# Routing and plan in measured parts beside the first expert units, all splits on VectorE in another order, and a drain of GpSimd

## The chip, the cores and the metric

The kernel runs on one core of a Trainium2 chip. The metric is the device time of one execution in microseconds (us), as the median of several runs. It takes 1409.32 us before the change (three runs, 1408.02 to 1411.92).

## What is computed

Three layers stand behind each other, all float32, for 4608 tokens of width 512:

```python
# attention with softmax over features (q) and over the sequence (k); x is [4608, 512]
kv = einsum('bhsd,bhse->bhde', k_s, v);  x = einsum('bhsd,bhde->bhse', q_s, kv)
# dense layer, 512 -> 2048 -> 512
r = maximum(x @ w_in, 0);  x = (s * (r * r) + b) @ w_out
# experts: 8, each 512 -> 1024 -> 512; a token goes to one of them
logits = xn @ en.T / tau;  expert_idx = argmax(logits);  gate = max of softmax(logits)
for e in range(8):
    h = maximum(x[mask] @ w1[e], 0);  out[mask] = gate[mask, None] * (h @ w2[e])
```

## The kernel before, in words

Precision: a float32 product is made of three matmuls in the fast type `float32r`: every operand is split into a high part (ScalarE copies and rounds it) and a low part (a subtraction, mostly on VectorE), and high x high, low x high and high x low are summed in PSUM. An expert's weights are split anew for each unit.

Stages: up to about 940 us the attention and the dense layer run in 12 blocks of 384 tokens. When a block of the dense layer is done, `route` (line 534) finds the expert of each of its tokens: 24 dot products on VectorE (3 groups of 128 tokens x 8 experts, lines 541 to 543), norms (with a power on GpSimd, line 504), the softmax, two small matmuls that count places (lines 579, 580), and three indirect DMAs from GpSimd that scatter (token, gate) into a table `tab` sorted by expert (line 597). `plan` (line 728) then works out which rows of the table and which expert each unit takes. `plan(True)` serves units 0 to 7 from the first 10 blocks and runs before the experts begin. `plan(False)` serves the later units and needs the routing of the last block (`NB - 1` = 11).

From 940 us on the expert stage runs 20 units, counted from 0 here and in the code: 18 units of 256 tokens (`FULL` = 18) and two of 128 tokens (units 18 and 19, `STAT` = 20), and more behind a condition that these inputs don't meet. A unit (`unit`, line 693) is two halves on TensorE. The first (L1, lines 688 to 690) has four quarters of 24 matmuls; each quarter's result goes through ScalarE (`hh`, line 704) and VectorE (`hl`, line 705) and then frees its PSUM buffer, of which there are two. The second half (L2, lines 715 to 717) has 48 matmuls. Between them `hook1(0..3)`, one behind each quarter of L1, and `hook2(0..3)`, at four places of L2, put the work for this unit's second weights and for the next unit into the engines' queues:

- `split(2, c)` (line 651): the four pieces of the second weights of this unit, 128 x 1024 each, a ScalarE copy (line 653) and a subtraction (line 654);
- `split(1, c)`: the four pieces of the first weights of the next unit;
- `emit_tr` (line 656): the 32 x 32 transposes of the next unit's tokens on VectorE (line 661), the ScalarE copy `xh` (line 664) and the VectorE subtraction `xl` (line 665);
- `gather` (line 622): two indirect DMAs from GpSimd that fetch the tokens of the unit after the next into `xr`;
- `deal` (line 630): 16 DMAs from SyncE that move `xr` into the layout `x` that the transposes read;
- `fetch_w1`, `fetch_w2`, `fetch_ids`: DMAs from SyncE; the weights' ones move nothing where the expert stays the same.

Each engine takes its queue in order. In the kernel before, `last_step` (line 1056) runs one step of the routing of block 11, and then of `plan(False)`, behind every hook, eight a unit: first one dot product a step, later the steps that the `yield`s in `route` and `plan` cut, with every third hook left out. While the routing runs, `split(2, 3)` has its subtraction on GpSimd, and until the plan is done `split(1, 0)` too. Unit 6 asserts that both are done, since `fetch_ids(8)` there reads the plan. `hook2` makes `split(1, i)` first and the transposes behind it, in `hook2(0)`, in unit 0 in `hook2(1)`. The first unit is begun early: `last_block` (line 964) loads, gathers, deals and splits for unit 0 beside the last dense block, and behind its last L1 (`m == NM`) does the first quarter of unit 0.

Of the kernel before, what the change touches and what calls it, by code (L numbers as in the profile page):

```python
# [8 lines left out]
F32 = mybir.dt.float32  # L9
# [4 lines left out]
ALU = mybir.AluOpType  # L14
# [7 lines left out]
E, F = 8, 1024  # L22
BT = 384
NB = NT // BT
# [8 lines left out]
FULL = 18  # L33
# [9 lines left out]
def attn_ffn_moe(ctx: ExitStack, tc: tile.TileContext, q, k, v, w_in, w_out, s_in, b_in,  # L43
# [490 lines left out]
    def route(t, nd=(3, 2)):  # L534
# [3 lines left out]
        for c in range(NC):  # L538
            yt = ysb.pop((t, c))
            for e in range(E):  # L540
                nc.vector.tensor_tensor_reduce(  # L541
                    out=junk_box[-1], in0=yt, in1=eb[:, e, :], scale=1.0, scalar=0.0,
                    op0=ALU.mult, op1=ALU.add, accum_out=dt[:, c, e:e + 1])
                n += 1
                if n == nd[k % len(nd)]:
                    n = 0
                    k += 1
                    yield
        nr = yield from norm_of(lp, sq, NC, "nr")
        nc.vector.reciprocal(out=nr, in_=nr)  # L550
        nc.vector.tensor_scalar(out=nr, in0=nr, scalar1=itau, scalar2=None, op0=ALU.mult)
        yield
        bc = lambda a: a.unsqueeze(2).to_broadcast([128, NC, E])
# [6 lines left out]
        ex = lp.tile([128, NC, E], F32, tag="ex", name="ex", bufs=1)  # L560
        nc.scalar.activation(out=ex, in_=dt, func=AF.Exp)

        pos = lp.tile([128, NC, E], F32, tag="pos", name="pos", bufs=1)
# [21 lines left out]
        ix = lp.tile([128, NC], I32, tag="ix", name="ix", bufs=2)  # L585
        nc.vector.tensor_copy(out=ix, in_=mx)
        nc.vector.tensor_tensor(out=cnt, in0=cnt, in1=pp[:, n3:n3 + E], op=ALU.add)
        py = lp.tile([128, NC, 2], I32, tag="py", name="py", bufs=2)
# [3 lines left out]
        nc.vector.tensor_copy(out=py[:, :, 0], in_=tok[:, NC * t:NC * t + NC])  # L592
        yield

# [7 lines left out]
        if t == NB - 1:  # L602
            list(scatter())
            yield
        else:
            prep.append(scatter())
# [5 lines left out]
    def parts_of(u):  # L612
        return 1 if FULL <= u < STAT else 2
# [36 lines left out]

    def split(n, c, eng=None):
        raw, hi, lo = moe[f"r{n}"][c], moe[f"h{n}"][c], moe[f"l{n}"][c]
        nc.scalar.activation(out=hi, in_=raw, func=AF.Copy)  # L653
        (eng or nc.vector).tensor_tensor(out=lo, in0=raw, in1=hi.bitcast(F32), op=ALU.subtract)  # L654

    def emit_tr(u):
        x, xf = moe["x"], moe["xf"]
        xh, xl = moe["xh"][u % 2], moe["xl"][u % 2]
        n = 128 * parts_of(u)
        xv = xf[:, :, 0:n]  # L660
        nc.vector.transpose(out=xv.rearrange("p c (g j) -> p g c j", j=32),
                            in_=x[:, 0:n // 32, :].rearrange("p g (c i) -> p g c i", c=KC))
        if n == UT:
            nc.scalar.activation(out=xh, in_=xv, func=AF.Copy)  # L664
            nc.vector.tensor_tensor(out=xl, in0=xv, in1=xh.bitcast(F32), op=ALU.subtract)  # L665
# [62 lines left out]
    def plan(first):  # L728
# [21 lines left out]
        for i in range(nb // E):  # L750
            nc.gpsimd.tensor_copy(out=eb[:, E * i:E * i + E], in_=eidx[0:1])
            nc.gpsimd.tensor_copy(out=rb[:, E * i:E * i + E], in_=segb[0:1])
        yield
        tt(out=c0, in0=cnt[0:1], in1=segb[0:1], op=ALU.subtract)
# [5 lines left out]
        cp(out=nu[:, 0:E], in_=ci)  # L760
        if not first:
            nc.vector.scalar_tensor_tensor(out=c0, in0=nu[:, 0:E], scalar=-float(UT), in1=c0,
                                           op0=ALU.mult, op1=ALU.add)
            ts(out=nu[:, E:], in0=c0, scalar1=0.0, scalar2=None, op0=ALU.is_gt)
            tt(out=rb[:, 0:E], in0=rb[:, 0:E], in1=eoff, op=ALU.add)
            nc.vector.scalar_tensor_tensor(out=rb[:, E:], in0=nu[:, 0:E], scalar=float(UT), in1=rb[:, 0:E],
                                           op0=ALU.mult, op1=ALU.add)
        yield

        for i in range(nb // E):  # L770
            src, dst = nu[:, E * i:E * i + E], c0
            for d in (1, 2, 4):
                a, z = slice(0, E - d), slice(d, E)
                o = hi[:, E * i:E * i + E] if d == 4 else dst
                if i == 0:
                    cp(out=o[:, E - d:E], in_=src[:, E - d:E])
                    tt(out=o[:, a], in0=src[:, a], in1=src[:, z], op=ALU.add)
                else:
                    cp(out=o[:, 0:d], in_=src[:, 0:d])
                    tt(out=o[:, z], in0=src[:, z], in1=src[:, a], op=ALU.add)  # L780
                src, dst = dst, c1
            if i:
                ts(out=hi[:, E:], in0=hi[:, E:], scalar1=hi[:, 0:1], scalar2=None, op0=ALU.add)
# [7 lines left out]
        nc.vector.scalar_tensor_tensor(out=rb, in0=lo, scalar=-float(UT), in1=rb, op0=ALU.mult, op1=ALU.add)  # L791
        yield
        tt(out=g3, in0=bu(uf), in1=be(lo), op=ALU.is_ge)
        tt(out=t3, in0=bu(uf), in1=be(hi), op=ALU.is_ge)
        tt(out=g3, in0=g3, in1=t3, op=ALU.subtract)
        nc.vector.tensor_reduce(out=va, in_=g3, axis=AX.X, op=ALU.add)
        tt(out=t3, in0=g3, in1=be(rb), op=ALU.mult)
        nc.vector.tensor_reduce(out=st, in_=t3, axis=AX.X, op=ALU.add)
        yield
        tt(out=t3, in0=g3, in1=be(eb), op=ALU.mult)  # L800
        nc.vector.tensor_reduce(out=ex[:, 1:], in_=t3, axis=AX.X, op=ALU.add)
        nc.vector.scalar_tensor_tensor(out=st, in0=uf, scalar=float(UT), in1=st, op0=ALU.mult, op1=ALU.add)

        ts(out=va, in0=va, scalar1=-2.0 * E * SEG, scalar2=2.0 * E * SEG, op0=ALU.mult, op1=ALU.add)
        tt(out=st, in0=st, in1=va, op=ALU.add)
        ts(out=st, in0=st, scalar1=float(E * SEG), scalar2=None, op0=ALU.min)
        yield
        ut = tp.tile([1, 3 * n + 3], I32, tag="ut" + tg, name="ut", bufs=1)
        u3 = ut[:, 0:3 * n].rearrange("p (n u) -> p n u", n=3)
        if first:  # L810
            nc.vector.memset(ex[:, 0:1], -1.0)
        else:
            cp(out=ex[:, 0:1], in_=ut_box[0][0:1, 2 * NA - 1:2 * NA])

            h0, h1 = FULL - NA, STAT - NA
            ts(out=c0[:, 0:2], in0=uf[:, h0:h1], scalar1=hi[:, 0:1], scalar2=None, op0=ALU.is_ge)
            ts(out=c1[:, 0:2], in0=c0[:, 0:2], scalar1=-float(E * SEG), scalar2=float(E * SEG),
               op0=ALU.mult, op1=ALU.add)
            tt(out=c1[:, 0:2], in0=c1[:, 0:2], in1=st[:, h0:h1], op=ALU.max)
            cp(out=ut[:, 3 * n:3 * n + 2], in_=c1[:, 0:2])  # L820
            ts(out=c0[:, 0:2], in0=c0[:, 0:2], scalar1=float(E * SEG), scalar2=None, op0=ALU.mult)
            tt(out=st[:, h0:h1], in0=c0[:, 0:2], in1=st[:, h0:h1], op=ALU.max)
            ts(out=c0[:, 0:1], in0=hi[:, 2 * E - 1:], scalar1=-2.0, scalar2=hi[:, 0:1], op0=ALU.add, op1=ALU.max)
            cp(out=ut[:, 3 * n + 2:], in_=c0[:, 0:1])
# [16 lines left out]
    with tc.manual_schedule():  # L841
# [97 lines left out]

        state = {}  # L940

# [22 lines left out]
        def last_block(m):  # L964
# [24 lines left out]
            if m == NM:  # L989
                early.append(unit_l1(0, 0))  # L990
            if m == NM + 1:
                xh, xl = rooms(2, F32R, "xh1", [128, KC, UT])
                moe["xh"].append(xh)
                moe["xl"].append(xl)
# [58 lines left out]

        steps = [0]

        def last_step():
            steps[0] += 1
            if steps[0] > NC * E and steps[0] % 3 == 0:
                return
            while last:  # L1060
                try:
                    next(last[0])
                    return
                except StopIteration:
                    last.pop(0)

        def run_unit(u, end):
# [4 lines left out]
            if more:  # L1072
                eg = fetch_w1(u + 1) if u + 1 != STAT - 1 else None
                if u + 2 < end:
                    fetch_ids(u + 2)

            def hook1(i):
                split(2, i, nc.gpsimd if len(last) > 1 and i == 3 else None)
                if i == 1 and more:
                    deal(u + 1)  # L1080
                if i == 3 and more:
                    if eg is not None:
# [3 lines left out]
                    if u + 2 == STAT - 1:  # L1086
# [4 lines left out]
                        load_w1(moe["e"], to="e1")  # L1091
                last_step()

            def trans():
                if more:
                    emit_tr(u + 1)
                    if u + 2 < end:
                        gather(u + 2)

            def hook2(i):  # L1100
                if more and parts_of(u + 1) == 2:
                    split(1, i, nc.gpsimd if last and i == 0 else None)
                if i == (1 if u == 0 else 0):
                    trans()
                last_step()

# [75 lines left out]
```

## Time and profile before

| | |
|---|---|
| median of 3 runs | 1409.32 us (1408.02 to 1411.92) |
| the profiled execution, time | 1407.17 us |
| the profiled execution, span from first to last instruction | 1405.4 us |
| busy: TensorE / VectorE / ScalarE / GpSimd | 1338.8 / 1008.0 / 889.4 / 173.1 us |
| mean granted TensorE clock | 0.983 |
| expert stage, first L1 of unit 1 to first L1 of unit 6 | 964.24 to 1093.48 us |

The profile is of one execution. In its rows an engine's busy time counts instructions; PE is TensorE, DVE VectorE, ACT ScalarE, POOL GpSimd and SP SyncE. A timeline row has the start, the length, the engine, the line, the operation with what it writes and reads, and in brackets the idle time before it and who ended it. `PEclk` is the granted clock, 1.00 being full speed. The letter q behind an engine's name stands for its queue: waits, branches, drains and DMA issues, which are not counted as busy.

### The profile page before, as it was taken

The page shows a single profiled execution, that of the slowest core. Times are in us where ns is not written, and L with a number is a line of the kernel's source. Part 1 is how long each engine was busy: PE and PEld are TensorE (multiplying, and loading weights), DVE is VectorE, ACT ScalarE, POOL GpSimd, SP SyncE. Part 2 cuts the span into 40 slices and gives each one's busy share as a digit, 9 for nine tenths or more (in the row PEclk, how much of TensorE's full clock was granted, in tenths as well). Part 3 has the DMA queues.
Part 4 walks back from the last instruction along what each step waited for, and adds up shares of the span by engine and source line. Part 5 has one row for each costly group of instructions (what it writes and reads, how often), then busy time and mean ns, then how long its engine had stood idle before and what let it go on. Part 6 is the DMA issues. An engine that isn't in the chain of part 4 may idle for free. (4 is left out here: it accounts for less than half of the span.)

```text
span 1405.4 us, 22783 instructions
## 1 busy us (share of the span) xinstructions
PE 1338.8 (95%) x7650; PEld 1181.1 (84%) x7650; DVE 1008.0 (72%) x2589; ACT 889.4 (63%) x1767; POOL 173.1 (12%) x170
## 2 busy tenths in 40 slices
PE   4898999999999999999999999998999999999995
PEld 2666888888888889888989988987888989899994
DVE  6886797878696969596969593647777666666642
ACT  5776767777676776677777675664554555555542
POOL 0000000000000000000010100113533221212110
PEclk9899999999999999999999999999999999999998
DMA  8641412121211121212111000412222222523332
GB/s 274 221 164 31 124 38 51 37 56 29 57 40 51 30 68 29 51 29 63 35 46 29 27 20 15 159 38 61 68 64 65 69 69 73 190 69 129 128 110 73
DMA packets 107456, 104.72 MB, mean 75 GB/s; under 512 B 55105, under 2 KB 83521, under 8 KB 107331
## 3 DMA queue, kind: packets, MB, share of 16 engines
q1 hardware_dynamic: 100098, 83.74, 20.3%
q0 software_dynamic: 7232, 19.44, 4.2%
q8 instruction: 62, 1.02, 0.3%
q14 instruction: 64, 0.52, 0.2%
HBM read 141.07 MB, written 19.73 MB: 114 GB/s over the span
## 5 line engine op out<-in xcount | busy, mean ns | idle before, releaser
L426 PE MATMUL ps_h<-xth,win 128*128 128x384 f32 x768 | 266.8, 347 | 0.8 <-ACT r L439 0.8
L427 PE MATMUL ps_h<-xtl,win 128*128 128x384 f32 x768 | 261.1, 340 | 0.0
L428 PE MATMUL ps_h<-xth,win 128*128 128x384 f32 x768 | 260.8, 340 | 0.0
L465 PE MATMUL ps_y<-wout,gl 128*128 128x512 f32 x534 | 210.9, 395 | 1.1 <-DVE gl L449 1.1
L466 PE MATMUL ps_y<-wout,gh 128*128 128x512 f32 x534 | 211.6, 396 | 0.0
L464 PE MATMUL ps_y<-wout,gh 128*128 128x512 f32 x534 | 210.0, 393 | 0.0
L654 DVE TENSOR_TENSOR l<-r,h 128x1024 fp32r<-128x1024 f32 x143 | 174.5, 1238 | 20.1 <-ACT h L653 17.4
L541 DVE CUSTOM_DVE_ANT_0 scr<-ysb,eb 128x512 bf16<-128x512 f32 x264 | 181.7, 688 | 5.8
L690 PE MATMUL ps_h<-xh,l 128*128 128x256 f32 x576 | 166.5, 289 | 7.5 <-DVE l L654 7.4
L449 DVE TENSOR_TENSOR gl<-r,gh 128x384 fp32r<-128x384 f32 x178 | 97.9, 550 | 100.9 <-ACT gh L447 98.9
L688 PE MATMUL ps_h<-xh,h 128*128 128x256 f32 x576 | 165.4, 287 | 2.6 <-ACT xh L664 1.8
L689 PE MATMUL ps_h<-xh,h 128*128 128x256 f32 x576 | 165.5, 287 | 1.1 <-DVE xh L665 1.1
L653 ACT ACTIVATE h<-r 128x1024 fp32r<-128x1024 f32 x152 | 155.7, 1050 | 0.0
L426 PEld LDWEIGHTS ps_h<-xth,win 128*128 128x128 f32 x768 | 145.6, 190 | 9.2 <-ACT r L439 1.6
L427 PEld LDWEIGHTS ps_h<-xtl,win 128*128 128x128 f32 x768 | 145.6, 190 | 5.3 <-issue 0.5
L428 PEld LDWEIGHTS ps_h<-xth,win 128*128 128x128 f32 x768 | 145.4, 189 | 0.0
L439 ACT ACTIVATE r<-ps_h 128x384 f32<-128x384 f32 x192 | 93.7, 488 | 80.5 <-PE ps_h L428 69.3
L446 ACT ACTIVATE r<-r,b_sb,s_sb 128x384 f32<-128x384 f32 x178 | 126.3, 709 | 5.9
L705 DVE SCALAR_TENSOR_TENSOR hl<-ps_h,hh 128x512 fp32r<-128x512 f32 x76 | 52.5, 691 | 104.5 <-ACT hh L704 94.0
L704 ACT ACTIVATE hh<-ps_h 128x512 fp32r<-128x512 f32 x76 | 45.4, 597 | 129.4 <-PE ps_h L690 117.1
L690 PEld LDWEIGHTS ps_h<-xh,l 128*128 128x128 f32 x576 | 112.7, 196 | 9.8 <-DVE l L654 9.8
L466 PEld LDWEIGHTS ps_y<-wout,gh 128*128 128x128 f32 x534 | 100.3, 188 | 23.0
(264 smaller groups left out, 2505.3 us busy)
## 6 DMA issues: line engine op xcount, KB each, us to landing
r<-moe_w SPq DMA_DIRECT2D x156, 512.0 KB
ysc<-ysb SPq DMA_DIRECT2D x36, 256.0 KB
x<-xr SPq DMA_DIRECT2D x288, 32.0 KB
qt_s<-q SPq DMA_DIRECT2D x45, 192.0 KB
rawin<-moe_w_in SPq DMA_DIRECT2D x16, 512.0 KB
rawout<-moe_w_out SPq DMA_DIRECT2D x16, 512.0 KB
kt_s<-k SPq DMA_DIRECT2D x29, 256.0 KB
vt_s<-v SPq DMA_DIRECT2D x29, 256.0 KB
```

The costliest lines, as they stand in the source:

```text
L426: nc.tensor.matmul(hp, wh[:, ws], xth[i][:, kk, :], start=(kk == 0), stop=False)
L427: nc.tensor.matmul(hp, wh[:, ws], xtl[i][:, kk, :], start=False, stop=False)
L428: nc.tensor.matmul(hp, wl[:, ws], xth[i][:, kk, :], start=False, stop=(kk == KC - 1))
L464: nc.tensor.matmul(y, g[:, cs], wh, start=(m == 0), stop=False)
L465: nc.tensor.matmul(y, l[:, cs], wh, start=False, stop=False)
L466: nc.tensor.matmul(y, g[:, cs], wl, start=False, stop=(m == NM - 1))
L541: nc.vector.tensor_tensor_reduce(out=junk_box[-1], in0=yt, in1=eb[:, e, :], scale=1.0, scalar=0.0, op0=ALU.mult, op1=ALU.add, accum_out=dt ...
L653: nc.scalar.activation(out=hi, in_=raw, func=AF.Copy)
L654: (eng or nc.vector).tensor_tensor(out=lo, in0=raw, in1=hi.bitcast(F32), op=ALU.subtract)
L688: nc.tensor.matmul(o, wh, xh[:, kk, :], start=(kk == 0), stop=False)
L689: nc.tensor.matmul(o, wh, xl[:, kk, :], start=False, stop=False)
L690: nc.tensor.matmul(o, wl, xh[:, kk, :], start=False, stop=(kk == KC - 1))
```

## The change

- `route` and `plan` yield a number now, and are cut into more steps. `last_step(room)` runs steps until the numbers have used up its room, or until a step yields nothing. It stands behind `hook1(1)`, `hook1(2)`, `hook1(3)` and `hook2(3)`, with rooms of 8, 8, 18 and 20. A dot product yields 8.
- No split runs on GpSimd any more.
- `hook1(0)` makes two splits of the second weights, `hook1(1)` and `hook1(2)` one each, `hook1(3)` none.
- `hook2(0)` makes the transposes first, `split(1, 0)` behind them, then `xh` and `xl`; `hook2(1..3)` make `split(1, 1..3)`. Unit 0 has no order of its own any more.
- `deal(1)` and `fetch_w1(1)` move from unit 0 to the last dense block, behind the first quarter of unit 0.
- A `drain` of GpSimd is put into `hook1(1)` of unit 17, the 18th.

```diff
@@ route
-                    yield
+                    yield 8
         nr = yield from norm_of(lp, sq, NC, "nr")
...
-        yield
+        yield 11
...
         nc.scalar.activation(out=ex, in_=dt, func=AF.Exp)
+        if t == NB - 1:
+            yield 8
...
         nc.vector.tensor_copy(out=ix, in_=mx)
+        if t == NB - 1:
+            yield 7
...
-        yield
+        yield 9
...
             list(scatter())
-            yield
+            yield 1
@@ split, emit_tr
-    def split(n, c, eng=None):
+    def split(n, c):
...
-        (eng or nc.vector).tensor_tensor(out=lo, in0=raw, in1=hi.bitcast(F32), op=ALU.subtract)
+        nc.vector.tensor_tensor(out=lo, in0=raw, in1=hi.bitcast(F32), op=ALU.subtract)
-    def emit_tr(u):
+    def emit_tr(u, beside=None):
...
         nc.vector.transpose(...)
+        if beside is not None:
+            beside()
         if n == UT:
@@ plan: its yields carry 1, 8, 5, 8, 6 now, and for the second plan there are new ones of 11, 9 (twice) and 8 (four times)
...
@@ last_block
             if m == NM:
                 early.append(unit_l1(0, 0))
+                deal(1)
+                early_w.append(fetch_w1(1))
@@ last_step, run_unit
-        def last_step():
-            steps[0] += 1
-            if steps[0] > NC * E and steps[0] % 3 == 0:
-                return
-            while last:
+        def last_step(room):
+            while last and room > 0:
                 try:
-                    next(last[0])
-                    return
+                    c = next(last[0])
                 except StopIteration:
                     last.pop(0)
+                    continue
+                if c is None:
+                    return
+                room -= c
...
-                eg = fetch_w1(u + 1) if u + 1 != STAT - 1 else None
+                eg = early_w.pop() if early_w else fetch_w1(u + 1) if u + 1 != STAT - 1 else None
...
             def hook1(i):
-                split(2, i, nc.gpsimd if len(last) > 1 and i == 3 else None)
-                if i == 1 and more:
+                for c in ((0, 1), (2,), (3,), ())[i]:
+                    split(2, c)
+                if i == 1 and more and u > 0:
                     deal(u + 1)
+                if i == 1 and u == FULL - 1:
+                    nc.gpsimd.drain()
...
-                last_step()
+                last_step((0, 8, 8, 18)[i])
...
-            def trans():
-                if more:
-                    emit_tr(u + 1)
+            def hook2(i):
+                full = more and parts_of(u + 1) == 2
+                if more and i == 0:
+                    emit_tr(u + 1, (lambda: split(1, 0)) if full else None)
                     if u + 2 < end:
                         gather(u + 2)
-            def hook2(i):
-                if more and parts_of(u + 1) == 2:
-                    split(1, i, nc.gpsimd if last and i == 0 else None)
-                if i == (1 if u == 0 else 0):
-                    trans()
-                last_step()
+                elif full:
+                    split(1, i)
+                if i == 3:
+                    last_step(20)
```

## Rows read from the trace of the kernel before

**Rows 1.** The page: busy time and share of the span of each engine.

```profile
PE 1338.8 (95%) x7650; PEld 1181.1 (84%) x7650; DVE 1008.0 (72%) x2589; ACT 889.4 (63%) x1767; POOL 173.1 (12%) x170
```

**Rows 2.** Windows by unit: from:to, length, busy PE PEld DVE ACT POOL, clock, DMA.

```profile
964.20:992.00 27.80, 25.75 (x145) 22.98 (x146) 21.92 (x32) 14.75 (x18) 11.59 (x8) 0.88 0.23 67
...
1064.20:1093.50 29.30, 26.02 (x146) 23.42 (x145) 22.70 (x42) 12.30 (x15) 5.49 (x4) 0.88 0.20 63
1093.50:1115.90 22.40, 22.40 (x145) 20.51 (x144) 14.66 (x15) 12.30 (x15) 5.05 (x4) 1.00 0.24 71
```

**Rows 3.** Timeline of TensorE: first L1 matmuls of units 1 to 6, and two waits.

```profile
964.24 0.38 PE L688 MATMUL ps_h<-xh,h 128*128 128x256 f32 x1 [1.81 <-ACT xh L664]
...
991.97 0.28 PE L688 MATMUL ps_h<-xh,h 128*128 128x256 f32 x1
...
1038.87 0.36 PE L688 MATMUL ps_h<-xh,h 128*128 128x256 f32 x1
...
1064.21 0.28 PE L688 MATMUL ps_h<-xh,h 128*128 128x256 f32 x1
...
1068.73 0.58 PE L690 MATMUL ps_h<-xh,l 128*128 128x256 f32 x1 [2.95 <-DVE l L654]
...
1093.48 0.28 PE L688 MATMUL ps_h<-xh,h 128*128 128x256 f32 x1
```

**Rows 4.** Waits of TensorE, 940 to 1090 us: total us, times, longest.

```profile
PE ps_h L690 <- DVE l L654: 7.4, 9, 2.9
PE ps_h L688 <- ACT xh L664: 1.8, 1, 1.8
```

**Rows 5.** Timeline of VectorE, 953 to 1120 us.

```profile
953.50 2.77 DVE L541 CUSTOM_DVE_ANT_0 junk<-ysb,eb 128x512 bf16<-128x512 f32 x1
...
961.85 1.25 DVE L661 STREAM_TRANSPOSE x<-x 128x1024 f32<-128x1024 f32 x1 [2.25 <-DMA r<-moe_w]
...
992.91 1.22 DVE L654 TENSOR_TENSOR l<-r,h 128x1024 fp32r<-128x1024 f32 x1
994.04 0.68 DVE L541 CUSTOM_DVE_ANT_0 junk<-ysb,eb 128x512 bf16<-128x512 f32 x1
994.65 0.08 DVE L541 DVE_READ_ACCUMULATOR2_ANT dots<- 128x1 f32 x1
...
1008.17 1.25 DVE L661 STREAM_TRANSPOSE x<-x 128x1024 f32<-128x1024 f32 x1 [1.57 <-DMA r<-moe_w]
...
1097.19 0.69 DVE L705 SCALAR_TENSOR_TENSOR hl<-ps_h,hh 128x512 fp32r<-128x512 f32 x1 [3.35 <-ACT hh L704]
...
1105.83 0.69 DVE L705 SCALAR_TENSOR_TENSOR hl<-ps_h,hh 128x512 fp32r<-128x512 f32 x1 [0.71 <-ACT hh L704]
1106.78 2.36 DVE L654 TENSOR_TENSOR l<-r,h 128x1024 fp32r<-128x1024 f32 x2 [0.26 <-ACT h L653]
```

**Rows 6.** Timeline of SyncE's queue: the 16 DMAs of a deal, units 2 and 4.

```profile
995.60 11.00 SPq L635 DMA_DIRECT2D x<-xr  x16
...
1044.41 12.38 SPq L635 DMA_DIRECT2D x<-xr  x16
```

**Rows 7.** Timeline of GpSimd: first and last scatter of block 11, a gather.

```profile
1046.46 0.97 POOL L597 DMA_INDIRECT tab<-py,ix  x1 [1.56 <-DVE hl L705]
...
1054.24 0.97 POOL L597 DMA_INDIRECT tab<-py,ix  x1 [2.79 <-DMA tab<-py,ix]
...
1108.43 1.58 POOL L626 DMA_INDIRECT xr<-ysc,ids  x1 [12.68 <-DMA r<-moe_w]
```

**Rows 8.** DMA view: indirect gathers, count, median us from issue to landing.

```profile
xr<-ysc,ids POOLq DMA_INDIRECT x38, 3.8
```

**Rows 9.** Timeline of TensorE, 1375 us: L1 of unit 19 and the wait before it.

```profile
1375.90 7.38 PE L680 MATMUL ps_h<-x,eb 128*128 128x128 f32 x64 [0.58 <-PE ps_y L717]
```

**Rows 10.** Drains in GpSimd's queue: the program's end (min/median/max ns), then its start.

```profile
L1141 POOLq DRAIN  x3: 45/107/9217, 1395.3 to 1405.1; - x3
...
L1136 POOLq DRAIN  x1: 169/169/169, 0.4 to 0.4; - x1
```

More of the change, by code (lines that the diff above doesn't have):

```diff
@@ L752, in plan @@
             nc.gpsimd.tensor_copy(out=rb[:, E * i:E * i + E], in_=segb[0:1])
-        yield
+        yield 1
         tt(out=c0, in0=cnt[0:1], in1=segb[0:1], op=ALU.subtract)
@@ L761, in plan @@
         if not first:
+            yield 11
+        if not first:
             nc.vector.scalar_tensor_tensor(out=c0, in0=nu[:, 0:E], scalar=-float(UT), in1=c0,
@@ L767, in plan @@
                                            op0=ALU.mult, op1=ALU.add)
-        yield
+        yield 8
         for i in range(nb // E):
@@ L781, in plan @@
                 src, dst = dst, c1
+            if not first:
+                yield 9
             if i:
@@ L791, in plan @@
         nc.vector.scalar_tensor_tensor(out=rb, in0=lo, scalar=-float(UT), in1=rb, op0=ALU.mult, op1=ALU.add)
-        yield
+        yield 5
         tt(out=g3, in0=bu(uf), in1=be(lo), op=ALU.is_ge)
         tt(out=t3, in0=bu(uf), in1=be(hi), op=ALU.is_ge)
+        if not first:
+            yield 8
         tt(out=g3, in0=g3, in1=t3, op=ALU.subtract)
         nc.vector.tensor_reduce(out=va, in_=g3, axis=AX.X, op=ALU.add)
+        if not first:
+            yield 8
         tt(out=t3, in0=g3, in1=be(rb), op=ALU.mult)
         nc.vector.tensor_reduce(out=st, in_=t3, axis=AX.X, op=ALU.add)
-        yield
+        yield 8
         tt(out=t3, in0=g3, in1=be(eb), op=ALU.mult)
         nc.vector.tensor_reduce(out=ex[:, 1:], in_=t3, axis=AX.X, op=ALU.add)
+        if not first:
+            yield 8
         nc.vector.scalar_tensor_tensor(out=st, in0=uf, scalar=float(UT), in1=st, op0=ALU.mult, op1=ALU.add)
@@ L806, in plan @@
         ts(out=st, in0=st, scalar1=float(E * SEG), scalar2=None, op0=ALU.min)
-        yield
+        yield 6
         ut = tp.tile([1, 3 * n + 3], I32, tag="ut" + tg, name="ut", bufs=1)
@@ L820, in plan @@
             cp(out=ut[:, 3 * n:3 * n + 2], in_=c1[:, 0:2])
+            yield 8
             ts(out=c0[:, 0:2], in0=c0[:, 0:2], scalar1=float(E * SEG), scalar2=None, op0=ALU.mult)
@@ L937, in attn_ffn_moe @@
         xtl.append(gp.tile([128, KC, BT], F32R, name="xtl1"))
-        state = {}
+        early_w = []
         def fetch_ids(u):
@@ L1052, in attn_ffn_moe @@
         last = [route(NB - 1, nd=(1,)), rest]
-        steps = [0]
-        def last_step():
-            steps[0] += 1
-            if steps[0] > NC * E and steps[0] % 3 == 0:
-                return
-            while last:
-                try:
-                    next(last[0])
-                    return
+        def last_step(room):
+            while last and room > 0:
+                try:
+                    c = next(last[0])
                 except StopIteration:
                     last.pop(0)
+                    continue
+                if c is None:
+                    return
+                room -= c
         def run_unit(u, end):
```

## The prediction

> **What bounds the kernel now.** The page comes first: TensorE is busy in 95% of the span, so what a change can win lies in its remaining waits, and in time that it spends at a lower clock [rows 1]. The windows cut by unit show where those are. Unit 6 fills its 22.4 us with 22.40 us of TensorE at full clock, while VectorE is busy in 14.66 us of them; unit 1 takes 27.8 and unit 5 takes 29.3 us for the same matmuls, both with a granted clock of 0.88 and VectorE at 22 us [rows 2]. The timeline gives the starts of L1: unit 1 at 964.24, unit 2 at 991.97, unit 4 at 1038.87, unit 5 at 1064.21, unit 6 at 1093.48 [rows 3]. A unit without waits takes 22.4 us [rows 2]; so units 1 to 5 lose 5.3, 2.1 (units 2 and 3 together), 2.9 and 6.9 us, 17.2 us in all, beside the 1.8 us in which unit 1's start waits. The waits view says on what: nine waits for the low parts of first weights, 7.4 us, and one for `xh`, 1.8 us [rows 4]. The rest up to 17.2 + 1.8 is mainly the clock: behind the waits of units 1 and 5 it fell to 1.2 GHz, and over 27.8 and 29.3 us a mean of 0.88 lacks 3.3 and 3.5 us. The chain is the same each time: VectorE's queue holds a dot product or a plan step ahead of each of the splits for which the next unit's first matmuls wait, or the transposes wait for their tokens, as at 961.85 [rows 5].
>
> **VectorE's load.** In units 1 and 2 it gets 8 dot products of 0.68 + 0.08 us [rows 5], 6.1 us, as before, and the two subtractions that GpSimd had, which are already in unit 6's 14.66 us. The sum, 20.8 us, is under 22.4, and overlapping ends make it less. The operations that ran beside GpSimd's subtractions get shorter: the dot product at 953.50 took 2.77 us [rows 5].
>
> **Its order.** I count from a unit's start S. In unit 6 the last `hl` begins at 1105.83, S + 12.35, and two splits behind it take 2.36 us, 1.14 each with the overlap [rows 5]. With two splits behind `hl(0)` instead of one, `hl(1)` starts some 0.3 us later; its PSUM buffer is wanted at S + 8.6, a us afterwards. Three dot products behind `hl(3)` end at about S + 15. Then come the transposes, `split(1, 0)`, `xl` and three splits, 6 x 1.14 plus 0.25 for a ScalarE copy: 7.1 us, to S + 22.2. The next L1 needs the fourth piece with its twelfth matmul, 0.12 us each, at S + 22.4 + 1.3. The slack is 1.5 us, and the three dot products behind end 2 us ahead of the next `hl(0)`, which stands 3.7 us behind that unit's start (1097.19 less 1093.48) [rows 3, 5]. So no matmul waits in units 1 to 3.
>
> **The tokens.** What could break this is a loop through SyncE. The last subtraction of the first weights ends at 994.13; the weights' DMAs, the ids and the 16 DMAs of a deal follow (995.60, 11.00 us long), and the transposes can go at 1008.17 [rows 5, 6]. (That row names a weights' DMA as its releaser; the transposes read `x` alone.) That is 14.0 us; with the 7.1 us from transposes to last subtraction the loop takes 21.1 us, under 22.4. Tokens come at S + 13.8, ahead of S + 15.
>
> **Unit 0.** `deal(1)` and `fetch_w1(1)` issue behind the transposes of unit 0, which free `x`, 11 us and 1.5 us, up to about 947 us. What stands behind them in SyncE's queue is three stores of the last block, which nothing needs for 100 us, `fetch_ids(2)`, and `fetch_w2`, which waits for unit 0's splits anyway. The tokens of unit 1 lie there at 947 instead of 961.85 [rows 5]. Unit 0's `hl(1)` now waits for a second split: up to 0.3 us on TensorE. Without its wait of 1.81 us unit 1 would start at 962.4; it starts at 962.7, 1.5 us earlier than now [rows 3].
>
> **Route's end and the plan.** Counting rooms, the dot products end with unit 2, the plan with `hook2(3)` of unit 5. Its short operations are hidden by VectorE's spare 7 us a unit. The scatter, in unit 4, now stands in `hook1(3)`: 1046.46 to 1055.21 us shows 8.8 us for its three DMAs [rows 7]. On GpSimd's queue it holds back the gather for unit 6, and the output DMAs, which have spare buffers. From S + 13.2 it ends at S + 22; the gather's two follow, 1.5 us each [rows 7], the second issued at S + 23.5, and land 3.8 us behind their issue [rows 8], at S + 27.3, 4.9 us into unit 5, where `deal(6)` waits on SyncE. With 11 us of DMAs and 1.5 us to land, the tokens come at 17.4, not 15; with 7.1 that is 24.5, where TensorE wants 23.7: about 0.8 us of wait at unit 6's start. In unit 6 `fetch_ids(8)` waits for the plan's last 2 us of VectorE behind the late splits, and `deal(7)` behind it; by the same sum unit 7 waits 0 to 1 us. I take 1.2 us for both, 0.8 and 0.4. The bounds are 0, if the gather lands as early as other deals start, and 4 us, if each of the five DMAs takes the longest spacing seen.
>
> **Units 6 to 17** are full of TensorE already [rows 2]; nothing is won there, and the new order hides under 7 us of spare VectorE. Unit 19's L1 waits 0.58 us now for its tokens [rows 9]; they are dealt earlier, and this goes: 0.6 us.
>
> **The drain.** At the end GpSimd's drain takes 9,217 ns, and the two behind it, with no DMA between, 107 and 45; the one at the program's start, before any indirect DMA, 169 [rows 10]. So its length follows what GpSimd did since the last one. Ahead of the long one stand 112 indirect DMAs (by the code 36 scatters, 38 gathers, 38 outputs). With a drain in unit 17 only 5 are left behind it (a gather, four outputs). If the cost is spread over them it is 0.08 us each, and the last drain takes 0.6 us: 8.6 us won. If any indirect DMA brings the whole cost, nothing is won. These are the bounds, 9.0 and 0. I take 8.6, since a cost that comes from work should grow with it. In unit 17 the drain holds the gather for unit 19 and that unit's outputs behind it, on a GpSimd that stood idle 12.68 us before such a gather [rows 7]; 9.2 us fit. Without that cover each us would delay the tokens of unit 19 by as much.
>
> The Trainium skill, "VectorE: DVE Perf Modes", section "The DRAIN you can't avoid", speaks against this part: the drains that open and close a program take a constant of about 12 ns on all five engines. Then there would be nothing to win, and the sum would be 1391.2 us, the time of rival 1. The trace does not agree, with 9,217 ns.
>
> **Sum.** 17.2 + 1.5 - 1.2 + 0.6 = 18.1 us in the experts, 8.6 us at the end: 26.7. The profiled execution took 1407.17 us for a span of 1405.4; it becomes 1380.5. The median lies 2.15 us over that execution, so on its scale 1409.32 - 26.7 = 1382.6.
>
> **Rivals.** (1) *The drain at the end stays long.* For it: the trace has no second long drain, so growth is not shown. Price: 8.6 us back, 1391.2. Chance 0.27. (2) *Half the waits stay:* one more operation of 1.5 us in VectorE's way, or the loop through SyncE with a deal of 12.38 us, as in unit 4 [rows 6], which makes it 22.5 us, and a fall of the clock behind the waits, as in units 1 and 5. 9 of the 18 us go: 1392 with the drain's gain, 1400 without. Chance 0.14. (3) *Slower, by the loop through SyncE:* with GpSimd's splits gone and VectorE nearly full, the deal alone sets the pace. Above 12.3 us a deal every unit is longer by the difference; to eat 18 + 9 us over the 17 units behind unit 1 it would have to reach 13.9 us. At 14.2 us the time is 1415. Against it: 11.0 us, and 12.38 at most [rows 6]. Chance 0.03. (4) *Nothing happens*, the waits only change places and the drain stays: 1409, 0.04. The forecast has 0.52.
>
> **The numbers.** 1382.6 us. The low end has both gains at their bounds (18.1 + 1.2 + 9.0) and the 1.3 us by which the lowest run lies under the median: 1379. The high end takes in rival 1 and half of rival 2's span: 1396. A measurement of this kernel can tell some 0.3% (4.2 us) from no change. Faster: 0.52 + 0.27 + 0.14 = 0.93; within: 0.04; slower: 0.03.
>
> **What would show it.** Right: L1 starts of units 1 to 6 at 22.4 us spacing from about 962.7, unit 6 near 1075.5; clock 1.00 in all windows there; no split on GpSimd; a wait of about a us at the first weights of units 6 or 7; a drain of about 9 us near 1327 us and a last one under 1 us. Wrong: transposes that wait for DMA in units 1 to 3 (the loop), VectorE waits ahead of `hl(0)`, a fallen clock, or a last drain that still takes 9 us.

## The result, and the profile after

The changed kernel takes 1384.47 us (median of four runs, 1382.47 to 1386.33), the kernel before 1409.28 us on the same chip: a ratio of 0.982, with a 95% interval of 0.980 to 0.984. That is 24.8 us less. The forecast was 26.7 us less, 1382.6 us. The profiled execution of after took 1384.38 us for a span of 1382.7.

The page's first part, to be held against [rows 1]:

```profile
PE 1334.4 (97%) x7650; PEld 1179.3 (85%) x7650; DVE 1003.6 (73%) x2598; ACT 890.5 (64%) x1767; POOL 146.2 (11%) x161
```

The windows by unit, here units 1, 5, 6 and 7 (columns as in [rows 2]):

```profile
965.40:987.80 22.40, 22.40 (x145) 20.52 (x144) 19.80 (x31) 12.31 (x15) 4.75 (x4) 1.00 0.25 71
...
1055.20:1077.60 22.40, 22.40 (x145) 20.52 (x144) 15.70 (x39) 9.22 (x12) 7.32 (x7) 1.00 0.35 74
1077.60:1104.80 27.20, 24.91 (x145) 22.14 (x145) 20.74 (x31) 15.27 (x19) 6.63 (x6) 0.94 0.27 86
1104.80:1127.20 22.40, 22.40 (x145) 20.51 (x145) 14.39 (x14) 12.42 (x15) 4.53 (x4) 1.00 0.25 72
```

Units 1 to 5 are full of TensorE at full clock now. One unit is not: unit 6 takes 27.2 us, 4.8 too many. TensorE's timeline, for [rows 3]: the first L1 of units 1, 2, 6 and 7, with the waits at unit 6's start, and that of unit 19, for [rows 9]:

```profile
965.39 0.28 PE L694 MATMUL ps_h<-xh,h 128*128 128x256 f32 x1
...
987.81 0.28 PE L694 MATMUL ps_h<-xh,h 128*128 128x256 f32 x1
...
1077.64 0.28 PE L694 MATMUL ps_h<-xh,h 128*128 128x256 f32 x1
1078.57 0.39 PE L695 MATMUL ps_h<-xh,h 128*128 128x256 f32 x1 [0.65 <-DVE xh L671]
...
1079.71 0.38 PE L696 MATMUL ps_h<-xh,l 128*128 128x256 f32 x1 [0.40 <-DVE l L658]
...
1081.04 0.39 PE L696 MATMUL ps_h<-xh,l 128*128 128x256 f32 x1 [0.71 <-DVE l L658]
...
1082.18 0.38 PE L696 MATMUL ps_h<-xh,l 128*128 128x256 f32 x1 [0.52 <-DVE l L658]
...
1104.86 0.28 PE L694 MATMUL ps_h<-xh,h 128*128 128x256 f32 x1
...
1364.08 0.38 PE L686 MATMUL ps_h<-x,eb 128*128 128x128 f32 x2
```

TensorE's waits from 940 to 1110 us, for [rows 4]. Nine waits on `l` have become three, all in unit 6, as is the one on `xh`. The one on `hl` stands in unit 0, and was as long before:

```profile
PE ps_h L696 <- DVE l L658: 1.6, 3, 0.7
PE ps_h L694 <- DVE hl L711: 0.8, 1, 0.8
PE ps_h L695 <- DVE xh L671: 0.7, 1, 0.7
```

VectorE in unit 2, for [rows 5]: the transposes, `split(1, 0)` in the time that ScalarE needs for `xh`, `xl`, the other three splits, and the next dot product:

```profile
1002.84 1.24 DVE L665 STREAM_TRANSPOSE x<-x 128x1024 f32<-128x1024 f32 x1
1004.00 1.18 DVE L658 TENSOR_TENSOR l<-r,h 128x1024 fp32r<-128x1024 f32 x1
1005.21 1.23 DVE L671 TENSOR_TENSOR xh<-x,xh 128x1024 fp32r<-128x1024 f32 x1
1006.35 3.69 DVE L658 TENSOR_TENSOR l<-r,h 128x1024 fp32r<-128x1024 f32 x3
1009.96 0.69 DVE L541 CUSTOM_DVE_ANT_0 junk<-ysb,eb 128x512 bf16<-128x512 f32 x1
```

Nothing there waits for tokens or for ScalarE. What makes unit 6 wait stands in three queues, from the second half of unit 4 on: GpSimd's scatters and gather, SyncE's deal, VectorE's transposes (for [rows 5 to 7]):

```profile
1045.96 0.97 POOL L601 DMA_INDIRECT tab<-py,ix  x1 [10.79 <-DVE py L596]
1049.84 1.70 POOL L601 DMA_INDIRECT tab<-py,ix  x1 [2.91 <-DMA tab<-py,ix]
1054.75 1.64 POOL L601 DMA_INDIRECT tab<-py,ix  x1 [3.21 <-DMA r<-moe_w]
1056.69 0.99 POOL L630 DMA_INDIRECT xr<-ysc,ids  x1 [0.30 <-issue]
1057.98 0.97 POOL L630 DMA_INDIRECT xr<-ysc,ids  x1 [0.30 <-issue]
...
1060.78 0.38 SPq L623 DMA_DIRECT2D ids<-tab  x1
1063.38 10.27 SPq L639 DMA_DIRECT2D x<-xr  x16
...
1074.92 1.25 DVE L665 STREAM_TRANSPOSE x<-x 128x1024 f32<-128x1024 f32 x1 [4.36 <-DMA x<-xr]
```

The scatters hold the deal in two ways. The gather stands behind them in GpSimd's queue, and the ids of unit 7, which SyncE fetches ahead of the deal, read the table that they write. By the waits of SyncE's queue `fetch_ids(7)` waited 4.2 us for the scatters, until 1060.78, and the deal behind it 2.2 us more for the gather. The gather ended last, but without it the ids alone would have kept the deal until about 1061.2, 6.0 us into unit 5 (an estimate, from the end of their issue).

GpSimd's queue at the end and in unit 17 (`L1101`), for [rows 10], with the semaphore update that stands ahead of the last drains:

```profile
L1101 POOLq DRAIN  x1: 10044/10044/10044, 1330.0 to 1330.0; - x1
...
L1131 POOLq INC_SWDGE_SEM  x1: 284/284/284, 1380.6 to 1380.6; - x1
...
L1160 POOLq DRAIN  x3: 51/107/606, 1381.2 to 1382.4; - x3
```

Of the 9.2 us at the end 0.6 us are left. The update was not in the prediction; in the kernel before it took 2,428 ns:

```profile
L1112 POOLq INC_SWDGE_SEM  x1: 2428/2428/2428, 1392.9 to 1392.9; - x1
```

The two profiles differ by 22.7 us of span, and the account closes. "Tail" is the time from the start of the last matmul (1388.36 before, 1376.46 after) to the span's end.

| part | before | after | won | forecast |
|---|---|---|---|---|
| up to unit 0's first L1 | 936.44 | 939.26 | -2.8 | 0 |
| unit 0 | 27.80 | 26.13 | 1.7 | 1.5 |
| units 1 to 5 | 129.24 | 112.25 | 17.0 | 17.2 |
| units 6 and 7 | 44.84 | 49.64 | -4.8 | -1.2 |
| unit 18, up to unit 19's first L1 | 13.38 | 12.60 | 0.8 | 0.6 |
| tail | 17.0 | 6.2 | 10.8 | 8.6 |

Units 8 to 17 take 22.42 us each in both, and unit 19 up to its last matmul the same to 0.1 us. The first line is no effect of the change: the code there is the same, and over all profiles of this study unit 0's first L1 stands between 936.4 and 939.8 us, in either kernel.

### The profile page after: what moved, and what is told of

It reads as the page before. It is cut to its first block, busy times and chain, and to the rows that moved or that the text cites. A ratio compares the mean times of both kernels' runs of the same rounds, so it can differ in the third digit from the quotient of the medians.

```text
span 1382.7 us, 22772 instructions
## 1 busy us (share of the span) xinstructions
PE 1334.4 (97%) x7650; PEld 1179.3 (85%) x7650; DVE 1003.6 (73%) x2598; ACT 890.5 (64%) x1767; POOL 146.2 (11%) x161
## 5 line engine op out<-in xcount | busy, mean ns | idle before, releaser
L658 DVE TENSOR_TENSOR l<-r,h 128x1024 fp32r<-128x1024 f32 x152 | 181.9, 1218 | 22.2 <-ACT h L657 21.2
L721 PE MATMUL ps_y<-h,hh 128*128 128x512 f32 x304 | 118.7, 390 | 0.0
L722 PE MATMUL ps_y<-h,hl 128*128 128x512 f32 x304 | 118.5, 390 | 0.0
```

The costliest lines, as they stand in the source:

```text
L658: nc.vector.tensor_tensor(out=lo, in0=raw, in1=hi.bitcast(F32), op=ALU.subtract)
```

## The experiments

### The drain, alone and left out

The kernel before with the drain alone:

```diff
             def hook1(i):
...
+                if i == 1 and u == FULL - 1:
+                    nc.gpsimd.drain()
```

> The kernel before with the drain in unit 17 as its only edit. Theory: the length of GpSimd's drain grows with the indirect DMAs since the last one (10.04 us for 107, 0.61 us for 5 in the changed kernel), and the semaphore update ahead of the last drain shortens with it (2.43 to 0.28 us). Then the last matmul stays where it is, within a us, the end comes 10.8 us sooner, and the time is 1398.5 us. Rival: the end is shorter only because of the other edits, or the drain in unit 17 holds up GpSimd where no change of order gives it room: 1405 to 1410 us, with the tokens of unit 19 late by some us.

Measured: 1397.43 us, ratio 0.9926 (0.9909 to 0.9942), 11.4 us less than before on the same chip. And the changed kernel without its drain:

```diff
-                if i == 1 and u == FULL - 1:
-                    nc.gpsimd.drain()
```

> The changed kernel without the drain. Theory: the last drain is 9 to 10 us long again and the update ahead of it 2.4 us, and nothing else changes: 1384.5 + 10.8 = 1395 us, unit starts within 0.1 us of the changed kernel's from unit 1 on. Rival: the shorter end comes from the subtractions that left GpSimd: the end stays at 6.2 us behind the last matmul and the time at 1384.5 us.

Measured: 1395.43 us, ratio 0.9902 (0.9886 to 0.9919). The drain is worth 11 us with the other parts and without them. Its part and theirs add up.

### A second drain, in unit 8

```diff
-                if i == 1 and u == FULL - 1:
+                if i == 1 and u in (8, FULL - 1):
                     nc.gpsimd.drain()
```

> The changed kernel with one more drain of GpSimd, in unit 8. Theory: a drain costs a fixed time for each indirect DMA since the last one, 0.08 to 0.093 us each: unit 8 about 6.7 us for some 72 of them, unit 17 about 3.3 us for some 35, the last 0.6 us. Rival: the length follows something else, the time run or the first drain's own cost; then the one in unit 17 is about 10 us again, or both are alike. The whole time should not move: 1384.

Measured: 1383.58 us in one run. The drains in unit 8 and unit 17, in GpSimd's queue, two stretches of one view:

```profile
L1101 POOLq DRAIN  x1: 7194/7194/7194, 1127.0 to 1127.0; - x1
...
L1101 POOLq DRAIN  x1: 4538/4538/4538, 1328.8 to 1328.8; - x1
```

In the order of the code 72 indirect DMAs stand ahead of the first and 35 between the two: 0.10 and 0.13 us each. In the changed kernel 107 stand ahead of 10,044 ns, 0.094 each. So a drain's length follows the indirect DMAs since the last one, and the rival (a fixed cost or the time run) falls; but not in exact proportion, since 35 were expected to cost 3.3 us. A likely reason stands in GpSimd's own rows: each of these drains begins while the output ahead of it has still to run, here in unit 17:

```profile
1329.03 0.99 POOL L728 DMA_INDIRECT out<-ot,ids  x1 [4.43 <-ACT ot L727]
```

From the drain's start to that output's end 1.2 us pass (1328.8 to 1330.02), and as much in the other two. Less 1.2 us the three are 6.0, 3.3 and 8.8 us, 0.083, 0.095 and 0.083 for each DMA, beside 0.082 for the 112 of the kernel before, whose last output ended long ahead. This is an estimate; no run takes the two parts apart.

### The scatters of block 11 two hooks earlier

Two stops of `route` ahead of the two small matmuls are gone for block 11, and the one ahead of the scatters ends its hook:

```diff
             nc.vector.tensor_tensor(out=ox[:, c + 1, :], in0=ox[:, c, :], in1=oh[:, c, :], op=ALU.add)
         yield
-        yield
-        if t == NB - 1:
+        if t < NB - 1:
             yield
...
         nc.vector.tensor_copy(out=py[:, :, 0], in_=tok[:, NC * t:NC * t + NC])
-        yield 9
+        yield
```

The scatters now go out in `hook1(1)` of unit 4, ahead of the gather and two hooks earlier than in the change.

> The changed kernel with the three scatters of block 11 one unit-third earlier: route gives them out in hook1(1) of unit 4, behind the ids of unit 6 and ahead of its gather, instead of hook1(3). Theory: unit 6 is 27.2 us long in place of 22.4 because the scatters stand ahead of the gather in GpSimd's queue, the tokens come 4.4 us late, and the clock falls behind the wait. Then the gather lands in time, unit 6 takes 22.4, and the whole 1379.7. Rival: the wait at unit 6 has another cause (the plan's steps on VectorE, the ids behind the plan); then 1384.5, as the change. Worse, if the scatters hold the ids or the gather somewhere else: over 1386.

Measured: 1379.97 us (five runs, 1377.98 to 1381.93), ratio 0.9789 (0.9775 to 0.9802): 4.5 us less than the change, and the lowest median of this study. Unit 6 in the windows, then the third scatter, the gather and the deal of unit 5:

```profile
1077.90:1100.30 22.40, 22.40 (x145) 20.52 (x144) 14.95 (x15) 12.30 (x15) 4.72 (x4) 1.00 0.24 73
```

```profile
1045.30 0.97 POOL L600 DMA_INDIRECT tab<-py,ix  x1 [2.94 <-DMA tab<-py,ix]
1050.14 0.99 POOL L629 DMA_INDIRECT xr<-ysc,ids  x1 [3.86 <-DMA x<-xr]
1051.43 1.22 POOL L629 DMA_INDIRECT xr<-ysc,ids  x1 [0.30 <-issue]
...
1058.19 10.94 SPq L638 DMA_DIRECT2D x<-xr  x16
```

The gather waits for its buffer alone, the deal starts at 1058.19, 3.0 us into unit 5 where the change has 8.2 (1063.38 less 1055.22), and the whole of the 4.8 us is gone. This settles that unit 6 waited for the scatters. It does not tell the gather from the ids, since the early scatters free both.

### `deal(1)` back in unit 0

```diff
             if m == NM:
                 early.append(unit_l1(0, 0))
-                deal(1)
-                early_w.append(fetch_w1(1))
...
-                if i == 1 and more and u > 0:
+                if i == 1 and more:
                     deal(u + 1)
```

> The changed kernel with deal(1) and fetch_w1(1) back in unit 0. Theory: most of what unit 1 lost before was that its tokens came late. They land at about 964.7 again, the fourth split of its first weights ends at about 971.8, behind the matmuls that want it; unit 1 begins late or waits in its first quarter, the clock falls behind the wait, and about 5 us go: 1390 to 1393. Rival: the early deal brought only the 1.5 us at unit 1's start that the prediction gave it, and the place of the dots brought the rest: 1386.

Measured: 1390.58 us, ratio 0.9865 (0.985 to 0.988), 6.1 us more than the change. The transposes of unit 1's tokens, and TensorE at its start:

```profile
965.39 1.25 DVE L665 STREAM_TRANSPOSE x<-x 128x1024 f32<-128x1024 f32 x1 [6.67 <-DMA r<-moe_w]
```

```profile
967.78 0.38 PE L694 MATMUL ps_h<-xh,h 128*128 128x256 f32 x1 [1.72 <-ACT xh L670]
969.04 0.58 PE L695 MATMUL ps_h<-xh,h 128*128 128x256 f32 x1 [0.88 <-DVE xh L671]
```

VectorE has no dot product or split left to do and stands idle for 6.67 us until the tokens are there (the row names a weights' DMA, but the transposes read `x` alone, and SyncE issued the last DMA of the deal at about 963.8); behind them unit 1 takes 27.21 us, with a granted clock of 0.87. That is the kernel before's unit 1 (27.73 us at 0.88 [rows 2, 3]), with none of its old order. What unit 1 lost were late tokens, and the fall of the clock behind them.

### The two subtractions back on GpSimd

```diff
-    def split(n, c):
+    def split(n, c, eng=None):
...
-                    split(2, c)
+                    split(2, c, nc.gpsimd if len(last) > 1 and c == 3 else None)
...
-                    emit_tr(u + 1, (lambda: split(1, 0)) if full else None)
+                    emit_tr(u + 1, (lambda: split(1, 0, nc.gpsimd if last else None)) if full else None)
```

> The changed kernel with the same subtractions on GpSimd as before: the fourth of the second weights while the routing runs, the first of the first weights until the plan is done. Theory (order): VectorE gets 2.3 us of work less a unit but its operations beside GpSimd's are held, a dot product 2.8 instead of 0.7 us and xl 3.4 instead of 1.2; the fourth split comes 0 to 2 us later, so units 1 to 5 take 22.4 to 24 us each, with no fall of the clock in unit 1: 1385 to 1390 us. Rival (GpSimd): most of the gain in units 1 to 5 came from taking these subtractions off GpSimd; then units 1 and 2 take 24 to 28 us with a fallen clock and the time is 1393 us or more.

Measured: 1390.72 us, ratio 0.9874 (0.9854 to 0.9894), 6.3 us more than the change, between the two bands. Units 1 to 5 take 23.70, 23.14, 23.13, 24.68 and 26.88 us: 9.3 us more than in the change. As the stage runs later, the gather behind the scatters is hidden better, and unit 6 gives 3.9 of it back (23.31 against 27.22). GpSimd's second subtraction and VectorE beside it, in unit 1:

```profile
979.82 2.55 POOL L658 TENSOR_TENSOR l<-r,h 128x1024 fp32r<-128x1024 f32 x1 [0.32 <-ACT h L657]
```

```profile
980.16 2.76 DVE L541 CUSTOM_DVE_ANT_0 junk<-ysb,eb 128x512 bf16<-128x512 f32 x1
...
982.96 0.69 DVE L541 CUSTOM_DVE_ANT_0 junk<-ysb,eb 128x512 bf16<-128x512 f32 x1
```

The dot product that starts beside it ends some 0.5 us behind it and takes 2.76 us in place of 0.69. A subtraction given to GpSimd saves VectorE 1.14 us and can hold it for 2.07. That is not the whole of the loss: of the 9.3 us 4.5 are unit 5's, where TensorE waits 2.71 us, at 1062.96, for GpSimd's subtraction itself, which stands behind the three scatters in its queue (1060.43), and the granted clock falls to 0.94.

### The kernel before with every subtraction on VectorE

```diff
-                split(2, i, nc.gpsimd if len(last) > 1 and i == 3 else None)
+                split(2, i)
...
-                    split(1, i, nc.gpsimd if last and i == 0 else None)
+                    split(1, i)
```

> The kernel before with its subtractions all on VectorE and nothing else changed. Theory: units 2 and 3 lost 1 us each because the two subtractions on GpSimd end late and slow what runs beside them on VectorE; they go to 22.4 us each, unit 1 keeps its late tokens (27.7 us or nearly so), units 4 and 5 gain a part of their 9.8 us: 1401 to 1407. Rival, the prediction's own first paragraph: dots and plan steps ahead of the splits in VectorE's queue were the cause; with two more subtractions there the waits grow: 1409 to 1415.

Measured: 1408.84 us (ten runs), ratio 0.9996 (0.9985 to 1.0007): nothing at all. My theory, 1401 to 1407, fell; the time lies just under the rival's lower end, 1409. Units 2 to 5 take 23.94, 24.00, 23.75 and 28.14 us where the kernel before has 23.45, 23.45, 25.34 and 29.27 [rows 3]. VectorE in unit 2:

```profile
1013.29 1.24 DVE L661 STREAM_TRANSPOSE x<-x 128x1024 f32<-128x1024 f32 x1
1015.66 1.23 DVE L665 TENSOR_TENSOR xh<-x,xh 128x1024 fp32r<-128x1024 f32 x1 [1.13 <-ACT xh L664]
...
1020.96 1.25 DVE L654 TENSOR_TENSOR l<-r,h 128x1024 fp32r<-128x1024 f32 x1
```

The transposes do not wait for tokens here, as they did before (1.57 us at 1008.17 [rows 5]): VectorE comes to them late by itself, and the fourth split ends at 1022.2, 2.7 us into the next unit, which starts at 1019.53. VectorE is held no longer, but has two more subtractions behind the last `hl`; one bound took the place of the other.

### The old order of splits, in the kernel with the early scatters

Both parts of the old order, on the kernel with the early scatters:

```diff
-                for c in ((0, 1), (2,), (3,), ())[i]:
-                    split(2, c)
+                split(2, i)
...
-                    emit_tr(u + 1, (lambda: split(1, 0)) if full else None)
+                    if full:
+                        split(1, 0)
+                    emit_tr(u + 1)
```

> The kernel with the early scatters (1379.97 us), with both parts of the old order of splits: one split of the second weights behind each quarter, and split(1,0) ahead of the transposes. Theory: VectorE's work behind hl(3) decides. In the changed kernel the fourth split of the first weights ends at S + 22.15 in unit 2, and the matmul wants it at about S + 23.7. The split of second weights behind hl(3) puts 1.4 us on it, and the idle 1.13 us in which VectorE waits for ScalarE's xh, now filled by split(1,0), another 1.1: S + 24.7, so that units 1 and 2 lose about 1 us each, and those with plan steps up to 2 each: 1383 to 1388. Rival: the order does nothing once GpSimd has no splits and the tokens are early: 1380.

Measured: 1386.88 us, ratio 0.9846 (0.9827 to 0.9865), 6.9 us more than its base. Units 1 to 4 take 23.67, 23.73, 23.74 and 23.75 us, with no fall of the clock. TensorE's waits up to 1110 us, and VectorE in unit 2:

```profile
PE ps_h L695 <- DVE l L657: 4.4, 11, 0.6
```

```profile
1005.58 1.24 DVE L664 STREAM_TRANSPOSE x<-x 128x1024 f32<-128x1024 f32 x1
1007.94 1.23 DVE L670 TENSOR_TENSOR xh<-x,xh 128x1024 fp32r<-128x1024 f32 x1 [1.13 <-ACT xh L669]
1009.09 3.69 DVE L657 TENSOR_TENSOR l<-r,h 128x1024 fp32r<-128x1024 f32 x3
```

The idle 1.13 us for `xh`, which the change fills with `split(1, 0)`, is back. With the first part alone, the transposes still ahead:

```diff
-                for c in ((0, 1), (2,), (3,), ())[i]:
-                    split(2, c)
+                split(2, i)
```

> The same kernel with one part of the old order alone: one split of the second weights behind each quarter, the transposes still ahead of split(1,0). Theory: 1.4 us more behind hl(3) make S + 23.55, which is still inside the slack of 1.5 us in units 1 to 3; only unit 5, 0.3 us long already, loses up to 1.4 us: 1380 to 1382. Rival: there is no slack, each unit with dots or plan steps loses 1 us or more: 1385 and over.

Measured: 1381.37 us, ratio 0.9809 (0.9789 to 0.9829), 1.4 us more than its base, which the two intervals don't tell from nothing. By the trace units 1 to 5 are 22.55 to 22.90 us long and unit 6 23.39, where the base has 22.41 to 22.74 and 22.42: the slack is used up, and overrun by 1.8 us in all six units together. The order as a whole is a bound, this part of it alone hardly. The other part alone, `split(1, 0)` ahead of the transposes, was not run.

### The dots between the splits again

The changed kernel with one step's room behind every hook:

```diff
-                last_step((0, 8, 8, 18)[i])
+                last_step(8)
...
-                if i == 3:
-                    last_step(20)
+                last_step(8)
```

> The changed kernel with room for one measured part behind every hook, so that the same eight dot products a unit stand between the splits as before. Theory (loop): three dot products between the transposes and the last split make this stretch 9.3 instead of 7.1 us; with 14.0 us from the last split through SyncE's 16 DMAs to the next transposes a unit takes 23.3 us, as units 2 and 3 took 23.45 before. Units 1 to 3 then lose 0.5 to 1 us each against the changed kernel, without a fall of the clock, and the time is 1386 to 1388 us. Rival: the place of the dot products does not matter as long as VectorE is under 22.4 us of work: 22.42 us a unit, 1384.5 us.

Measured: 1395.32 us, ratio 0.9907 (0.9887 to 0.9927), 10.9 us more than the change, but not where the dots are: units 1 to 3 take 22.42, 22.42 and 22.58 us. Units 4 and 5 take 28.30 and 30.61, unit 5 at a granted clock of 0.80. SyncE and TensorE at unit 5's start:

```profile
1047.59 0.39 SPq L623 DMA_DIRECT2D ids<-tab  x1
1048.09 10.24 SPq L639 DMA_DIRECT2D x<-xr  x16
...
1062.10 0.58 PE L694 MATMUL ps_h<-xh,h 128*128 128x256 f32 x1 [5.40 <-ACT xh L670]
```

With other rooms the scatters come 11.5 us earlier, at 1034.43, ahead of `fetch_ids(6)`. Those ids read the table that the scatters write, so SyncE holds them until 1047.59, and the deal behind them with them. It is the second of the two ways that the change shows in unit 5, here by itself. The dots' place cost nothing in the three units that this run shows, and the loop through SyncE that I expected to reach 23.3 us did not show itself; whether it would over more units stays open.

## Why the prediction was right, and where it was wrong

**Units 1 to 5**, 17.2 us: right in size (17.0) and in part wrong in cause. The first paragraph said that the chain is the same each time, a dot product or a plan step ahead of each split, or late tokens. Late tokens it was, in unit 1; but dots between the splits cost nothing in units 1 to 3 once the rest is in place. That GpSimd's subtractions hold VectorE's operations the prediction said in passing and gave no price. Three conditions must hold together, and each one undone alone costs 6 to 7 us: early tokens for unit 1 (6.1), no subtraction on GpSimd (6.3; units 1 to 5 alone lose 9.3, about half of it to a subtraction behind the scatters), the order behind the last `hl` (6.9, in the kernel with the early scatters). The second one alone, put into the kernel before, brings nothing (0.9996): the other two still hold the same units. Those were not tried alone there.

**Unit 0**, 1.5 us: the term measured 1.7 in its own unit, but `deal(1)` was worth 6.1. Its larger part was booked under units 1 to 5, with no word on how much of those is late tokens. The row that says so was at hand: the transposes of unit 1 waited 2.25 us [rows 5].

**The order** came out to a few tenths. The fourth split was put at S + 22.2 and ends at S + 22.15 in unit 2 (the dot product behind it starts at 1009.96; S is 987.81); the slack of 1.5 us is what the last two order runs found: 1.4 us just about fit, 2.5 don't.

**The loop through SyncE**, 21.1 us: no transposes of units 1 to 4 wait for it. Right.

**Units 6 and 7**, 1.2 us: the one term that failed, 4.8 us in this profile, above its bound of 4. The mechanism was right as far as it went (the scatters hold the gather, the deal waits), as the run with early scatters shows, but it left out the ids, which hold the deal too. Three sizes were wrong. The deal starts 8.2 us into unit 5, not 4.9: the scatters took 10.4 us (1045.96 to 1056.39), not 8.8, and the deal starts 5.4 us behind the issue of the second gather (1057.98), not 3.8. And beside waits of 2.3 us TensorE was busy 2.5 us longer, 24.91 us in place of 22.40. About 1.6 of these are the granted clock: it stood at 0.50, 1.2 GHz, from 1083 to 1086, and its mean of 0.94 lacks 1.6 us of 27.2. The rest comes with the waits, as the run with two drains shows, which has the same code up to there: unit 6 has 2.1 us of waits there, no fall of the clock, and takes 25.60 us, 3.2 too many. So of the 4.8 us about 3.2 are the waits and 1.6 the clock, and it is the clock that takes the term over its bound. Without the drain unit 6 takes 28.15 us, at 0.88. The sum left the clock out, and had the row for it: units 1 and 5 at 0.88 [rows 2]. Unit 7 waits for nothing.

**The drain**, 8.6 us: 0.6 us was forecast for the last one and 606 ns came. The tail won 10.8, since the semaphore update ahead of it shrank from 2,428 to 284 ns as well. Rival 1, which had 0.27, falls, and with it what the Trainium skill, "VectorE: DVE Perf Modes", section "The DRAIN you can't avoid", would make of it: drains of about 12 ns that stay constant. GpSimd's took 606 to 10,044 ns with the work before them.

**Sum.** The miss at unit 6 (3.6 us) and the larger tail (2.2 us) went against each other; so 1384.5 lies near 1382.6 partly by luck.

## What to carry to other kernels

Where several chains end within a us of each other, the wait that the trace names is only the last of them: undo each part of a change by itself, in the new kernel as well as in the old one, before one of them gets the credit. A step moved to another place takes its DMAs past other queues: look for the one that waits for data written by a slow DMA ahead of it (here scatter, table, ids, deal). And price a wait on TensorE above its own length, with the clock that may fall behind it: here waits of 2.1 to 2.3 us cost unit 6 3.2 us without a fall and 4.8 with one.

## What the runs showed of the hardware

A drain of GpSimd pays for the indirect DMAs since the last one, about 0.1 us each (7,194 ns for 72, 10,044 for 107, 606 for 5), and it can be paid while the rest of the core works; TensorE lost nothing in unit 17, which takes 22.42 us. What of such a DMA it pays for stays open.

VectorE operations on two operands in SBUF stood still beside a GpSimd subtraction: 2.76 us in place of 0.69 for a dot product, and in the kernel before even a subtraction of 128 x 24 elements:

```profile
1029.72 2.39 POOL L654 TENSOR_TENSOR l<-r,h 128x1024 fp32r<-128x1024 f32 x1 [6.41 <-ACT h L653]
...
1029.96 2.18 DVE L559 TENSOR_TENSOR dots<-dots,mx 128x24 f32<-128x24 f32 x1
```

The same line takes 0.18 us in the run with all subtractions on VectorE. The Trainium skill, "SBUF — State Buffer", section "SBUF: two separate sides", gives the rule: VectorE and GpSimd share one pair of ports, which a VectorE instruction with two inputs in SBUF needs beside a GpSimd one that reads SBUF; the one that starts first holds the pair for its whole instruction, and the other stands still. The trace agrees: GpSimd's subtraction starts 0.24 us ahead and ends at 1032.11, VectorE's small one at 1032.14.
